# Attention scores and the folded projection as 64x32 TensorE blocks in place of half-empty 128x64 blocks

## The chip, the cores and the metric

The kernel runs on one core of a Trainium2 chip. The metric is the device time of one execution in microseconds. A kernel's time is the median of its runs, given with the lowest and the highest. Line numbers such as L177 are lines of the kernel that the profile is of, so the same statement has other numbers in other kernels.

## The reference, cut to what matters

There are 8 batches of 8 heads, 512 tokens and 32 state vectors of 64 elements each. The model has 512 columns and the hidden layer 2048. The weights come as fp64 and the kernel decodes them to fp32 itself.

```python
B, H, S, Ns, D = (8, 8, 512, 32, 64)
scores = scale * np.matmul(x, state.transpose(0, 1, 3, 2))
a = softmax(scores)                      # cut: max, exp, sum + 1e-9
xread = np.matmul(a, state)
scores2 = scale * np.matmul(state, x.transpose(0, 1, 3, 2))
a2 = softmax(scores2)
sread = np.matmul(a2, x)
# ... concatenated, heads side by side: 512 columns, then
h = x @ w_in
g = np.where(h > 0.0, h, np.exp(np.minimum(h, 0.0)) - 1.0)
return g @ w_out
```

## The kernel before

The read of the tokens is never formed. Since `xread @ w_in` is `a @ (state @ w_in)`, the kernel computes for each batch M = state x w_in (256 rows of head and state, 2048 columns) and multiplies it by the transposed softmax weights. M is made in four chunks of 512 columns; TensorE does that between the matmuls of the first feed-forward layer (`h_ps`).

Scores and M use the same stationary operand. Before the change it lay zero-padded in `k_bd`: the transposed states of four heads were put on two diagonals, so that one matmul takes all 128 partitions (two heads of 64) and 64 columns, half of which are zero for each head.

```python
def scores(b, g):
    ps = bank([P, S], "s_ps")
    for i in range(2):
        nc.tensor.matmul(ps[i * D : (i + 1) * D],
            k_bd[:, b * G + g, i * D : (i + 1) * D], st[b, g, i], ...)
    # ... two softmaxes: over the states and over the tokens

def make_m(b, c):
    m_t[b, c] = mpool.tile([P, G, 512], FP32, name="m_sb")
    for g in range(G):
        ps = bank([P, 512], "m_ps")
        for i in range(2):
            nc.tensor.matmul(ps[i * D : (i + 1) * D],
                k_bd[:, b * G + g, i * D : (i + 1) * D],
                w_in[:, 2 * g + i, c * 512 : (c + 1) * 512], ...)
        (nc.scalar.copy, nc.vector.tensor_copy)[g % 2](out=m_t[b, c][:, g], in_=ps)
# ... the main loop, for each batch b:
#     16 groups of ffn1 (h_ps), with M's chunks 1 to 3 of this batch and the attention
#     of batch b + 1 put between them,
#     then 4 groups of ffn2 (o_ps), with M's chunk 0 of batch b + 1 between them
```

`bank` takes one of three PSUM banks; `h_ps` has three of its own and `o_ps` two. At the start, the state came in 4 loads on GpSimd's queue, `x` on the sync queue and GpSimd's, and the weights on the sync queue.

Of the kernel before, what the change touches and what calls it, by code (L numbers as in the profile page):

```python
# [9 lines left out]
FP32 = mybir.dt.float32  # L10
# [9 lines left out]
def kernel(  # L20
# [11 lines left out]
    nc = tc.nc  # L32

    B, H, S, D = x.shape
    NS = state.shape[2]
    DM, DF = moe_w_in.shape
    P = 128
    R = S // P
    NP = H // 2
    G = H // 4  # L40
    FO = DF // P
    FC = DF // 512
    SB = S + NS
# [14 lines left out]
    apool = ctx.enter_context(tc.tile_pool(name="attn", bufs=2))  # L58
    xtpool = ctx.enter_context(tc.tile_pool(name="xT", bufs=4))
    atpool = ctx.enter_context(tc.tile_pool(name="aT", bufs=4))  # L60
    mpool = ctx.enter_context(tc.tile_pool(name="m", bufs=2))
    rawpool = ctx.enter_context(tc.tile_pool(name="raw", bufs=3))
    wpool = ctx.enter_context(tc.tile_pool(name="pow", bufs=2))
# [8 lines left out]
    def bank(shape, name):  # L72
        return ps_a.tile(shape, FP32, tag="a", name=name)
# [5 lines left out]
    w_in = cpool.tile([P, NP, DF], FP32, name="w_in")  # L79
    w_out = cpool.tile([P, FO, DM], FP32, name="w_out")  # L80


    v_bd = cpool.tile([P, B * G, P], FP32, name="v_bd")

    k_bd = cpool.tile([P, B * G, P], FP32, name="k_bd")

    xT_state = cpool.tile([P, NP, B * NS], FP32, name="xT_state")

# [8 lines left out]
            )  # L97

    def setup():
        nc.vector.memset(v_bd, 0.0)  # L100
        make_identity(nc, ident)
        s_v = state.rearrange("b (g h) n d -> h n (b g) d", h=4)
        for h in range(4):
            c = h % 2
            nc.gpsimd.dma_start(
                out=v_bd[h * NS : (h + 1) * NS, :, c * D : (c + 1) * D], in_=s_v[h]
            )
        for b in range(2):
            load_x(b)
        for k in range(0, B * G, 4):  # L110
            ps = bank([P, 4, P], "k_ps")
            for i in range(4):
                nc.tensor.transpose(ps[:, i], v_bd[:, k + i], ident)  # L113
            nc.vector.tensor_copy(out=k_bd[:, k : k + 4], in_=ps)  # L114

    def load_weights(dst, src):

# [41 lines left out]
    def load_w_out(fo):  # L159
        load_weights(w_out[:, fo : fo + 1], w_out_v[:, fo : fo + 1])  # L160

    def turn_x(b, g, i):

        ps = bank([P, R, P], "xT_ps")
        for r in range(R):
            nc.tensor.transpose(ps[:, r], x_t[b][:, r, (2 * g + i) * P : (2 * g + i + 1) * P], ident)  # L166
        st[b, g, i] = xtpool.tile([P, R * P], FP32, name="xT")
        nc.scalar.copy(out=st[b, g, i], in_=ps.rearrange("p r q -> p (r q)"))  # L168

    def scores(b, g):  # L170


        ps = bank([P, S], "s_ps")
        for i in range(2):
            nc.tensor.matmul(  # L175
                ps[i * D : (i + 1) * D],
                k_bd[:, b * G + g, i * D : (i + 1) * D],  # L177
                st[b, g, i],
                start=True,
                stop=True,  # L180
            )
        top = small.tile([P, 1], FP32, name="top")
        total = small.tile([P, 1], FP32, name="total")
        nc.vector.reduce_max(top, ps, axis=AX_X)
# [35 lines left out]
    def turn_state(b, g):  # L220
        ps = bank([P, R, P], "sT_ps")
        a = st[b, g, "a_s"].rearrange("p (r q) -> p r q", r=R)
        for r in range(R):
            nc.tensor.transpose(ps[:, r], a[:, r], ident)  # L224
        st[b, g, "aT_s"] = apool.tile([P, R, P], FP32, name="aT_s")
        nc.scalar.copy(out=st[b, g, "aT_s"], in_=ps)  # L226

    def state_read(b, g):

        ps = bank([P, 2, 2 * NS], "sr_ps")  # L230
        for i in range(2):
            for r in range(R):
                nc.tensor.matmul(  # L233
                    ps[:, i],
                    x_t[b][:, r, (2 * g + i) * P : (2 * g + i + 1) * P],
                    st[b, g, "aT_s"][:, r, i * D : (i + 1) * D],
                    start=(r == 0),
                    stop=(r == R - 1),
                )
        for c in range(2):  # L240
            rows = slice(c * D, (c + 1) * D)
            nc.vector.tensor_copy(  # L242
                out=xT_state[rows, 2 * g : 2 * g + 2, b * NS : (b + 1) * NS],
                in_=ps[rows, :, c * NS : (c + 1) * NS],
            )

    def make_m(b, c):

        m_t[b, c] = mpool.tile([P, G, 512], FP32, name="m_sb")
        for g in range(G):  # L250
            ps = bank([P, 512], "m_ps")
            for i in range(2):
                nc.tensor.matmul(  # L253
                    ps[i * D : (i + 1) * D],
                    k_bd[:, b * G + g, i * D : (i + 1) * D],
                    w_in[:, 2 * g + i, c * 512 : (c + 1) * 512],
                    start=True,
                    stop=True,
                )
            (nc.scalar.copy, nc.vector.tensor_copy)[g % 2](out=m_t[b, c][:, g], in_=ps)  # L260

    def attention(b):
        steps = []
        for g in range(G):
            steps += [lambda g=g, i=i: turn_x(b, g, i) for i in range(2)]
            steps += [lambda g=g: scores(b, g)]
        for g in range(G):
            steps += [lambda g=g: turn_tokens(b, g)]
            steps += [lambda g=g: turn_state(b, g)]
            steps += [lambda g=g: state_read(b, g)]  # L270
        if b + 2 < B:
            steps += [lambda: load_x(b + 2)]
        return steps
# [59 lines left out]
    for b in range(B):  # L333
        todo = attention(b + 1) if b + 1 < B else []
        g = {}
# [62 lines left out]
```

## Time and profile before

| What | Before |
|---|---|
| time, median of 4 runs (lowest to highest) | 932.17 us (931.69 to 932.48) |
| span of the profiled run | 931.1 us |
| steady period, from one batch's last `o_ps` matmul to the next batch's | 99.15 us, five times |
| the first batch's last `o_ps` matmul starts | 196.8 us |
| first weight decode begins, last one ends | 15.24 us, 165.4 us |

The periods are read from the starts of the `o_ps` matmuls in the trace; below, "the first batch ends" means the start of its last one. Two stages matter: up to about 165 us VectorE decodes the weights, and from there TensorE is full. So a saving on TensorE counts in the second stage only. This is the chain of waits at the start (start, duration, engine, what; SPq is the issue queue of SyncE, L95 loads x and L121 the raw weights):

```profile
0.74 0.45 SPq L95
...
2.71 0.97 SPq L95
...
3.72 2.93 SPq L121
...
6.69 11.91 DMA raw<-in_moe_w_in_dram
...
18.63 0.43 DVE power L126
```

Only four issues of x stand ahead of the weights, so the first weights are asked for at 3.72 us. In the chain of waits (start, duration, engine, what) VectorE takes up the second of the weights at 18.63 us.

### The profile page before, as it was taken

What the parts mean: (1) busy time and instruction counts of PE and PEld (TensorE: products, weight loads), DVE (VectorE), ACT (ScalarE), POOL (GpSimd) and SP (SyncE); (2) the same over time, 40 slices, a digit from 0 to 9 for tenths busy, and PEclk for the clock granted to TensorE, in tenths of its full rate; (3) what the DMA queues carried; (4) which work ended last, traced back from release to release, by engine and by line L of the source; (5) the groups of instructions that cost most, each with busy time, mean ns of one, the idle gap of its engine ahead of it and who ended that gap; (6) DMA issues with size and microseconds to landing.
All of it is one profiled execution on the core that took longest, in us unless ns stands there. A gap on an engine that the chain in (4) does not pass through costs nothing.

```text
span 931.1 us, 6560 instructions
## 1 busy us (share of the span) xinstructions
PE 872.7 (94%) x2512; PEld 401.3 (43%) x2512; DVE 363.1 (39%) x774; ACT 156.9 (17%) x290; POOL 53.1 (6%) x58
## 2 busy tenths in 40 slices
PE   1474999999999999999999999999999999999997
PEld 1331443445444444444444444454444444444673
DVE  3989999435004610272017400660036102500220
ACT  0211211123003300141004200330023101300110
POOL 3110110001000200010001000000001000000000
PEclk9966999999999999999999999999999999999999
DMA  8354242002000110002000200000000000000000
GB/s 200 109 148 153 90 136 91 23 23 46 1 23 23 25 21 23 23 0 46 23 23 0 46 23 1 23 1 1 23 24 0 1 23 23 0 1 23 23 0 23
DMA packets 25439, 35.01 MB, mean 38 GB/s; under 512 B 17857, under 2 KB 17857, under 8 KB 25409
## 3 DMA queue, kind: packets, MB, share of 16 engines
q1 hardware_dynamic: 23936, 29.89, 10.4%
q0 software_dynamic: 1472, 4.72, 2.3%
q8 instruction: 19, 0.31, 0.1%
q14 instruction: 12, 0.09, 0.0%
HBM read 25.69 MB, written 8.91 MB: 37 GB/s over the span
## 4 chain that ended last, share of the span: by engine, by line
PE 88%; DVE 8%; DMA 3%; SPq 1%; ACT 0%; issue 0%; POOL 0%; DVEq 0%; ACTq 0%
PE o_ps L315 49%; PE h_ps L290 23%; PE m_ps L253 6%; PE h_ps L303 3%; DMA raw<-in_moe_w_in_dram 3%; PE sr_ps L233 3%; PE s_ps L175 2%; PE xT_ps L166 2%; DVE power L139 1%; DVE w_in L148 1%; DVE power L126 1%; DVE raw L144 1%; PE sT_ps L224 1%; DVE power L131 1%; DVE power L135 1%; DVE w_in L151 0%
## 5 line engine op out<-in xcount | busy, mean ns | idle before, releaser
L315 PE MATMUL o_ps<-w_out,g_sb 128*128 128x512 f32 x1088 | 473.6, 594 | 0.0
L315 PEld LDWEIGHTS o_ps<-w_out,g_sb 128*128 128x128 f32 x1088 | 205.3, 190 | 263.0 <-issue 256.3
L290 PE MATMUL h_ps<-aT,m_sb 128*128 128x512 f32 x512 | 242.1, 606 | 12.8 <-DVE m_sb L260 12.6
L290 PEld LDWEIGHTS h_ps<-aT,m_sb 128*128 128x128 f32 x512 | 92.3, 193 | 123.1 <-issue 82.7
L279 ACT ACTIVATE e_sb<-h_ps 128x512 f32<-128x512 f32 (+1 forms) x144 | 82.4, 572 | 335.4 <-PE h_ps L290 295.9
L322 DVE COPY o_sb<-o_ps 128x512 f32<-128x512 f32 x17 | 11.7, 690 | 323.6 <-PE o_ps L315 323.6
L282 DVE SCALAR_TENSOR_TENSOR g_sb<-e_sb,h_ps 128x512 f32<-128x512 f32 (+1 forms) x144 | 93.7, 651 | 11.6 <-PE o_ps L315 8.6
L280 DVE TENSOR_SCALAR e_sb<-e_sb 128x512 f32<-128x512 f32 (+1 forms) x144 | 59.0, 410 | 98.4 <-ACT e_sb L279 98.4
L253 PE MATMUL m_ps<-w_in,k_bd 128*64 128x512 f32 x256 | 68.1, 622 | 1.5 <-ACT xT L168 0.8
L322 ACT COPY o_sb<-o_ps 128x512 f32<-128x512 f32 x17 | 10.0, 586 | 304.5 <-PE o_ps L315 304.5
L260 DVE COPY m_sb<-m_ps 128x512 f32<-128x512 f32 x32 | 22.0, 688 | 91.0 <-PE m_ps L253 89.5
L199 POOL TENSOR_TENSOR t_sb<-t_sb,top_t 128x512 f32<-128x512 f32 x16 | 17.8, 1115 | 570.0 <-DVE top_t L198 445.4
L233 PEld LDWEIGHTS sr_ps<-aT_s,x_sb 128*128 128x128 f32 x256 | 33.9, 209 | 10.9 <-ACT aT_s L226 6.4
L253 PEld LDWEIGHTS m_ps<-w_in,k_bd 128*64 128x64 f32 x256 | 15.8, 138 | 46.5 <-issue 35.3
L233 PE MATMUL sr_ps<-aT_s,x_sb 128*128 128x64 f32 x256 | 34.5, 292 | 1.4 <-ACT aT_s L226 1.3
L113 PE MATMUL k_ps<-ident,v_bd 128*128 128x128 f32 x16 | 3.9, 426 | 29.8 <-DVE k_bd L114 16.6
L303 PE MATMUL h_ps<-xT_state,w_in 128*128 128x256 f32 x128 | 27.8, 379 | 0.0
L168 ACT COPY xT<-xT_ps 128x512 f32<-128x512 f32 x32 | 18.6, 584 | 52.6 <-PE xT_ps L166 52.6
L166 PEld LDWEIGHTS xT_ps<-ident,x_sb 128*128 128x128 f32 x128 | 16.6, 151 | 22.5 <-issue 12.1
L303 PEld LDWEIGHTS h_ps<-xT_state,w_in 128*128 128x128 f32 x128 | 24.3, 190 | 3.7 <-issue 0.5
L166 PE MATMUL xT_ps<-ident,x_sb 128*128 128x128 f32 x128 | 21.4, 295 | 3.1 <-DVE xT_state L242 3.0
L260 ACT COPY m_sb<-m_ps 128x512 f32<-128x512 f32 x32 | 18.8, 586 | 22.9 <-PE m_ps L253 22.9
(42 smaller groups left out, 328.7 us busy)
## 6 DMA issues: line engine op xcount, KB each, us to landing
raw<-in_moe_w_in_dram SPq DMA_DIRECT2D x16, 512.0 KB, 4.2
raw<-in_moe_w_out_dram SPq DMA_DIRECT2D x16, 512.0 KB, 3.3
out_dram<-o_sb SPq DMA_DIRECT2D x16, 512.0 KB, 2.6
x_sb<-in_x_dram SPq DMA_DIRECT2D x16, 256.0 KB, 4.8
x_sb<-in_x_dram POOLq DMA_DIRECT2D x16, 256.0 KB, 5.9
v_bd<-in_state_dram POOLq DMA_DIRECT2D x4, 128.0 KB, 7.6
out_dram<-o_sb SPq DMA_DIRECT2D x8, 64.0 KB, 1.7
```

The lines of the kernel that those rows point to most:

```text
L166: nc.tensor.transpose(ps[:, r], x_t[b][:, r, (2 * g + i) * P : (2 * g + i + 1) * P], ident)
L175: nc.tensor.matmul(ps[i * D : (i + 1) * D], k_bd[:, b * G + g, i * D : (i + 1) * D], st[b, g, i], start=True, stop=True,)
L233: nc.tensor.matmul(ps[:, i], x_t[b][:, r, (2 * g + i) * P : (2 * g + i + 1) * P], st[b, g, "aT_s"][:, r, i * D : (i + 1) * D], start=(r == 0),
L253: nc.tensor.matmul(ps[i * D : (i + 1) * D], k_bd[:, b * G + g, i * D : (i + 1) * D], w_in[:, 2 * g + i, c * 512 : (c + 1) * 512], start=Tr ...
L260: (nc.scalar.copy, nc.vector.tensor_copy)[g % 2](out=m_t[b, c][:, g], in_=ps)
L279: nc.scalar.activation(out=e, in_=ps, func=AF.Exp)
L280: nc.vector.tensor_scalar(out=e, in0=e, scalar1=1.0, scalar2=None, op0=ALU.min)
L282: nc.vector.scalar_tensor_tensor(out=g[fo], in0=e, scalar=-1.0, in1=ps, op0=ALU.add, op1=ALU.max)
L290: nc.tensor.matmul(ps, m_t[b, fo // 4][:, k, fo % 4 * P : (fo % 4 + 1) * P], st[b, k, "aT"], start=(k == 0), stop=(k == G - 1),)
L303: nc.tensor.matmul(ps, w_in[:, co, fo * P : (fo + 1) * P], xT_state[:, co], start=(co == 0), stop=(co == NP - 1),)
L315: nc.tensor.matmul(ps, g[fo][:, c * P : (c + 1) * P], w_out[:, fo], start=(fo == 0), stop=(fo == FO - 1),)
L322: (nc.scalar.copy, nc.vector.tensor_copy)[c % 2](out=o_sb[:, c % 2], in_=ps)
```

## The change

The change regroups the heads by their place in the pair. The transposed states lie densely in `kT` (two heads of 64 partitions, 32 columns per batch), and each head's product is one block of 64 rows by 32 columns of TensorE's array. Eight such blocks, one for each head, fill the array. The intent is that all eight run side by side, in half of the time that the zero-padded blocks took.

```diff
-    def scores(b, g):
-        ps = bank([P, S], "s_ps")
-        for i in range(2):
-            nc.tensor.matmul(
-                ps[i * D : (i + 1) * D],
-                k_bd[:, b * G + g, i * D : (i + 1) * D],
-                st[b, g, i],
...
+    def by_state(b, name, rhs):
+        ps = [bank([P, 512], name) for g in range(G)]
+        for m in range(NP):
+            for g in range(G):
+                d = slice(g * D, (g + 1) * D)
+                nc.tensor.matmul(
+                    ps[g][m * NS : (m + 1) * NS],
+                    kT[d, m, b * NS : (b + 1) * NS],
+                    rhs[m][d],
+                    start=True,
+                    stop=True,
+                    tile_position=(g * D, m * NS),
+                )
+        return ps
+
+    def scores(b):
+        for g, ps in enumerate(by_state(b, "s_ps", [st[b, m] for m in range(NP)])):
+            softmaxes(b, g, ps)
...
     def make_m(b, c):
-        for g in range(G):
-            ps = bank([P, 512], "m_ps")
...
+        cols = slice(c * 512, (c + 1) * 512)
+        for g, ps in enumerate(by_state(b, "m_ps", [w_in[:, m, cols] for m in range(NP)])):
```

The setup of the state changes with it, and the two state reads of a batch become one:

```diff
     def setup():
-        nc.vector.memset(v_bd, 0.0)
...
-        s_v = state.rearrange("b (g h) n d -> h n (b g) d", h=4)
-        for h in range(4):
-            c = h % 2
-            nc.gpsimd.dma_start(
-                out=v_bd[h * NS : (h + 1) * NS, :, c * D : (c + 1) * D], in_=s_v[h]
-            )
+        s_v = state.rearrange("(q b) (m c) n d -> q m b n c d", q=2, c=2)
+        raw = [rawpool.tile([P, NP, P], FP32, tag="raw", name="s_sb") for q in range(2)]
+        for q in range(2):
+            for m in range(NP):
+                for b in range(B // 2):
+                    (nc.sync, nc.gpsimd)[q].dma_start(
+                        out=raw[q][b * NS : (b + 1) * NS, m].rearrange("p (c d) -> p c d", c=2),
+                        in_=s_v[q, m, b],
+                    )
         for b in range(2):
             load_x(b)
-        for k in range(0, B * G, 4):
+        for q in range(2):
...
```

More of the change, by code (lines that the diff above doesn't have):

```diff
@@ L39 @@
     NP = H // 2
-    G = H // 4
+    G = 2
     FO = DF // P
@@ L60 @@
     atpool = ctx.enter_context(tc.tile_pool(name="aT", bufs=4))
+    atspool = ctx.enter_context(tc.tile_pool(name="aT_s", bufs=1))
     mpool = ctx.enter_context(tc.tile_pool(name="m", bufs=2))
@@ L80 @@
     w_out = cpool.tile([P, FO, DM], FP32, name="w_out")
-    v_bd = cpool.tile([P, B * G, P], FP32, name="v_bd")
-    k_bd = cpool.tile([P, B * G, P], FP32, name="k_bd")
+    kT = cpool.tile([P, NP, B * NS], FP32, name="kT")
     xT_state = cpool.tile([P, NP, B * NS], FP32, name="xT_state")
@@ L99, in setup @@
     def setup():
-        nc.vector.memset(v_bd, 0.0)
         make_identity(nc, ident)
-        s_v = state.rearrange("b (g h) n d -> h n (b g) d", h=4)
-        for h in range(4):
-            c = h % 2
-            nc.gpsimd.dma_start(
-                out=v_bd[h * NS : (h + 1) * NS, :, c * D : (c + 1) * D], in_=s_v[h]
-            )
+        s_v = state.rearrange("(q b) (m c) n d -> q m b n c d", q=2, c=2)
[7 more added lines that the diff above has]
+                    )
         for b in range(2):
             load_x(b)
-        for k in range(0, B * G, 4):
-            ps = bank([P, 4, P], "k_ps")
-            for i in range(4):
-                nc.tensor.transpose(ps[:, i], v_bd[:, k + i], ident)
-            nc.vector.tensor_copy(out=k_bd[:, k : k + 4], in_=ps)
+        for q in range(2):
+            ps = bank([P, NP, P], "k_ps")
+            for m in range(NP):
+                nc.tensor.transpose(ps[:, m], raw[q][:, m], ident)
+            nc.vector.tensor_copy(out=kT[:, :, q * P : (q + 1) * P], in_=ps)
     def load_weights(dst, src):
@@ L160, in load_w_out, with turn_x, softmaxes @@
         load_weights(w_out[:, fo : fo + 1], w_out_v[:, fo : fo + 1])
-    def turn_x(b, g, i):
+    def turn_x(b, m):
         ps = bank([P, R, P], "xT_ps")
         for r in range(R):
-            nc.tensor.transpose(ps[:, r], x_t[b][:, r, (2 * g + i) * P : (2 * g + i + 1) * P], ident)
-        st[b, g, i] = xtpool.tile([P, R * P], FP32, name="xT")
-        nc.scalar.copy(out=st[b, g, i], in_=ps.rearrange("p r q -> p (r q)"))
-    def scores(b, g):
-        ps = bank([P, S], "s_ps")
-        for i in range(2):
-            nc.tensor.matmul(
-                ps[i * D : (i + 1) * D],
-                k_bd[:, b * G + g, i * D : (i + 1) * D],
-                st[b, g, i],
-                start=True,
-                stop=True,
-            )
+            nc.tensor.transpose(ps[:, r], x_t[b][:, r, m * P : (m + 1) * P], ident)
+        st[b, m] = xtpool.tile([P, R * P], FP32, name="xT")
+        nc.scalar.copy(out=st[b, m], in_=ps.rearrange("p r q -> p (r q)"))
+    def by_state(b, name, rhs):
+        ps = [bank([P, 512], name) for g in range(G)]
+        for m in range(NP):
+            for g in range(G):
[12 more added lines that the diff above has]
+            softmaxes(b, g, ps)
+    def softmaxes(b, g, ps):
         top = small.tile([P, 1], FP32, name="top")
@@ L224, in turn_state, with state_read @@
             nc.tensor.transpose(ps[:, r], a[:, r], ident)
-        st[b, g, "aT_s"] = apool.tile([P, R, P], FP32, name="aT_s")
-        nc.scalar.copy(out=st[b, g, "aT_s"], in_=ps)
-    def state_read(b, g):
-        ps = bank([P, 2, 2 * NS], "sr_ps")
-        for i in range(2):
+        if g == 0:
+            st[b, "aT_s"] = atspool.tile([P, R, G, P], FP32, name="aT_s")
+        nc.scalar.copy(out=st[b, "aT_s"][:, :, g], in_=ps)
+    def state_read(b):
+        ps = bank([P, NP, G, NS], "sr_ps")
+        for m in range(NP):
             for r in range(R):
                 nc.tensor.matmul(
-                    ps[:, i],
-                    x_t[b][:, r, (2 * g + i) * P : (2 * g + i + 1) * P],
-                    st[b, g, "aT_s"][:, r, i * D : (i + 1) * D],
+                    ps[:, m],
+                    x_t[b][:, r, m * P : (m + 1) * P],
+                    st[b, "aT_s"][:, r, :, m * NS : (m + 1) * NS],
                     start=(r == 0),
@@ L239, in state_read @@
                 )
-        for c in range(2):
-            rows = slice(c * D, (c + 1) * D)
+        for g in range(G):
+            rows = slice(g * D, (g + 1) * D)
             nc.vector.tensor_copy(
-                out=xT_state[rows, 2 * g : 2 * g + 2, b * NS : (b + 1) * NS],
-                in_=ps[rows, :, c * NS : (c + 1) * NS],
+                out=xT_state[rows, :, b * NS : (b + 1) * NS], in_=ps[rows, :, g]
             )
@@ L249, in make_m @@
         m_t[b, c] = mpool.tile([P, G, 512], FP32, name="m_sb")
-        for g in range(G):
-            ps = bank([P, 512], "m_ps")
-            for i in range(2):
-                nc.tensor.matmul(
-                    ps[i * D : (i + 1) * D],
-                    k_bd[:, b * G + g, i * D : (i + 1) * D],
-                    w_in[:, 2 * g + i, c * 512 : (c + 1) * 512],
-                    start=True,
-                    stop=True,
-                )
+        cols = slice(c * 512, (c + 1) * 512)
+        for g, ps in enumerate(by_state(b, "m_ps", [w_in[:, m, cols] for m in range(NP)])):
             (nc.scalar.copy, nc.vector.tensor_copy)[g % 2](out=m_t[b, c][:, g], in_=ps)
@@ L263, in attention @@
         steps = []
-        for g in range(G):
-            steps += [lambda g=g, i=i: turn_x(b, g, i) for i in range(2)]
-            steps += [lambda g=g: scores(b, g)]
+        steps += [lambda m=m: turn_x(b, m) for m in range(NP)]
+        steps += [lambda: scores(b)]
         for g in range(G):
@@ L269, in attention @@
             steps += [lambda g=g: turn_state(b, g)]
-            steps += [lambda g=g: state_read(b, g)]
+        steps += [lambda: state_read(b)]
         if b + 2 < B:
```

## The prediction

Four words are used in it and below. A pass is one run of the moving columns through TensorE's array; the trace has two passes for each fp32 product. A slot is the 430 ns between the starts of two full-array passes of 512 columns. An excursion is a stretch of passes in smaller blocks between full-array ones, and its toll is what it costs beyond its slots.

> **What bounds the kernel now.** I read the page's busy times first, then the slices, then the stretches of time by engine, then the chain of waits in order of time.
>
> The page, busy times and slices:
>
> ```profile
> PE 872.7 (94%) x2512; PEld 401.3 (43%) x2512; DVE 363.1 (39%) x774; ACT 156.9 (17%) x290; POOL 53.1 (6%) x58
> PE   1474999999999999999999999999999999999997
> DVE  3989999435004610272017400660036102500220
> PEclk9966999999999999999999999999999999999999
> ```
>
> From the fifth slice (93 us) TensorE (PE) is full; before that VectorE (DVE) is. The stretches of one later batch and of the start, by engine:
>
> ```profile
> 70.00:80.00 10.00, 0.81 (x2) 0.00 (x0) 9.61 (x21) 0.00 (x0) 0.00 (x0) 0.50 0.46 145
> 130.00:140.00 10.00, 10.00 (x25) 3.23 (x24) 9.91 (x24) 1.78 (x3) 0.00 (x0) 1.00 0.45 155
> 369.00:468.00 99.00, 99.00 (x289) 44.24 (x288) 30.43 (x64) 18.43 (x34) 6.04 (x6) 1.00 0.08 22
> ```
>
> The columns after the width are PE, weight load, DVE, ScalarE (ACT), GpSimd. So there are two stages: up to about 142 us DVE decodes the fp64 weights and sets the pace; after it PE never idles, DVE has two thirds of its time free, and a nanosecond off PE's sequence is a nanosecond off the time. The chain of waits repeats every 99.15 us there (batch 3's `h_ps` starts at 287.01, batch 4's at 386.16). The chain around one tiled stretch:
>
> ```profile
> 401.44 1.87 PE m_ps L253 x8
> 403.31 0.86 PE s_ps L175 x4
> 404.17 3.63 PE h_ps L290 x8
> ```
>
> and the groups that the change touches:
>
> ```profile
> L253 PE MATMUL m_ps<-w_in,k_bd 128*64 128x512 f32 x256 | 68.1, 622 | 1.5 <-ACT xT L168 0.8
> L175 PE MATMUL s_ps<-xT,k_bd 128*64 128x512 f32 x64 | 20.1, 641 | 1.6 <-ACT xT L168 1.6
> ```
>
> 622 ns is a latency, not what one costs. I took starts of single matmuls from the trace. An fp32 matmul is two passes. Full-array passes of 512 columns start 430 ns apart. In an M stretch the passes start at 413.658 and 413.665, then 414.138 and 414.145, 414.567 and 414.574, 414.997 and 415.003: the two 64-column blocks of a pair run together, 7 ns apart. So today M (8 passes) is 4 slots of 430 ns and scores of one group (4 passes) are 2 slots.
>
> Around each such excursion there is a toll: entry takes 522 instead of 430 ns (+92), its first pass waits for its weights (643 against 592 ns, +51), the second block starts 7 later, the exit takes 523 (+93), and the next full pass waits for its weights (697 against 592, some +100). About 0.343 us per excursion.
>
> **What the Trainium skill says.** "TensorEngine Tiling (Array Packing)", section Tiling Modes: 64x32 gives 8 independent tiles, and changing the mode drains the array; the +92 and +93 ns agree. Its section Restrictions and Gotchas: two row tiles may not write one PSUM bank together; the new code gives each half of a pair its own bank. "TensorE: Matmul & The Clock Gate", section Part 3: a packed group takes one matmul plus some 4 ns per further tile, measured up to 16 tiles at 10.6 times; it also says matmuls start strictly in program order. The trace shows 7 ns per block, and disagrees on order: in the compiled program each block's two passes stand next to each other, yet the second block's first pass starts (413.665) before the first block's second (414.138). This matters: with strict order, eight blocks of two passes would take nine slots. The same page, LDWEIGHTS (loading the stationary operand): columns / 1.2 ns, so 53 for 64 and 107 for 128; the trace's +51 and +105 agree, and 27 for 32 columns is an estimate from it.
>
> **The change part by part.**
>
> (1) Slots. M becomes 8 blocks of 64x32, two passes each, all in different tiles. If all eight run together, M is 2 slots instead of 4, and the scores of a batch 2 instead of 2x2. Per batch of the steady stage: before 4 M (16) + 2 scores (4) = 20 slots = 8.60 us; after 4x2 + 2 = 10 slots, if nothing is split.
>
> (2) Excursions. The order in which the built programs' instructions stand shows five of them per steady batch before (one joins M and scores) and six after: three whole Ms, the scores by themselves, and one M split into its first block and the other seven with an `h_ps` between. A single block still needs 2 slots, so the split adds them: 12 slots = 5.16 us. The toll of one is 0.343 - 0.024 (shorter weights) + 0.042 (six more blocks at 7 ns) = 0.361.
> Before: 8.60 + 5 x 0.343 = 10.32 us. After: 5.16 + 6 x 0.361 = 7.33 us. Gain 2.99 us.
>
> (3) A new wait. The two score banks now fill at once, and the next M needs two of the three banks of that pool after one `h_ps` of 4 passes only. Its second bank is the first score bank, which is free when ACT's exponential has read it. With scores starting at 0: `h_ps` before it ends at 0.1, ACT's ELU at 0.7, DVE's minimum and g at 1.7, DVE's maximum at 2.4, transpose issued 2.3, negated maximum 3.0, exponential 3.05 to 3.74 (durations 0.60, 0.43, 0.69, 0.69, 0.71, 0.15, 0.69 from the timeline). PE arrives there at 1.03 (scores over) + 0.10 + 4 x 0.43 + 0.09 = 2.94. So M's second block waits some 0.85 us, and I find 0.15 more at the transpose of the state weights that takes the second score bank. About 1.0 us per batch is given back. The state read in one run of 32 passes instead of two of 16 saves one entry, 0.1.
> Net per steady batch 2.99 - 1.0 + 0.1 = 2.1 us, over five such batches 10.4 us.
>
> (4) The last batch's period has only four Ms: before 16 x 0.43 + 4 x 0.343 = 8.25, after 8 x 0.43 + 4 x 0.361 = 4.88: 3.4 us.
>
> (5) Batch 0. Up to about 142 us DVE paces, so PE's saving is mostly idle time there. Of the excursions behind that point I count 7 with some 20 slots (11.0 us) before, and 8 with 16 slots (9.8 us) after: 1 us.
>
> (6) Start. Removed: memset of `v_bd` (1.77 us of DVE, beside the wait for the first weights, free), two of four copies of 0.6 us (on DVE's path: 1.2 us). Added: 32 small state loads for 4. On the sync queue 16 issues at some 0.4 us (0.315 to 0.44 is what small ones take) stand ahead of x and the weights, and two of the three raw buffers are held until the state is transposed. The first decode starts at 15.24 us now and the second weights come at 18.63; I estimate the first at about 17.5, the following close behind, with both k copies already done. Two fewer state copies per batch give DVE 0.4 us each. Net about 1 us better, plus or minus 3, since the batch-2 loads of x also stand differently among the weight loads, where DVE loses some 4.5 us today (50 to 76 us).
>
> Sum: 10.4 + 3.4 + 1 + 1 = 15.8 us. 932.2 - 15.8 = 916.4; I say 916.
>
> **The rivals.**
> *Strict order or a short look-ahead.* The trace proves only that one waiting pass can be overtaken; eight blocks need up to seven. With pairs only, M takes about 8 to 9 slots, a steady batch 41 slots and more: 17.9 + 2.2 = 20 against 10.3 us, some +60 us in all, 990. For it: the skill's sentence on order. Against: the 7 ns starts, and its 16-tile measurement. 7%.
> *Only column tiles or only row tiles run together.* Four slots per M: 22 slots and six excursions, 11.6 us, +1.3 and the bank wait per batch: about 944. 6%.
> *No bank wait.* If DVE and ACT serve the scores sooner than my walk says, 5 us more come: 911. The single place where my working is finest is this 0.85 us.
> *More bank wait.* DVE now gets both softmaxes of a batch in a burst (about 8.6 us of DVE work within some 13 us, with ELU at 1.1 us per 1.72 between); a further 1 us per batch at `h_ps`, waiting for g to free its bank, would make 921.
> *The start.* The state loads could delay everything by 5 us (921), or the weight loads could fit better (912).
>
> **Range and chances.** The PE sum is arithmetic on slots that the trace repeats to the nanosecond; the uncertain terms are the bank wait (0 to 2 us, five times), the start (plus or minus 4) and whether eight run together. The 2% line is at 913.5, 2.5 us below my number. So: range 907 to 929, chance faster 0.34, same 0.59, slower 0.07.
>
> **What would show it.** In a steady batch the period should fall from 99.15 to about 97. The trace should show eight first passes within some 50 ns, the eight second passes one slot later, and an M excursion near 0.96 us from first start to exit instead of 1.87. PE should show a new idle, on ACT's `a_s` reading `s_ps` (L204), just under 1 us per batch. The first weight decode should start at 16 to 19 us. PE should still be 90% busy or more from 100 us on. I am wrong if first passes come in twos or fours with slots between them, if PE's idle per batch exceeds 2 us, or if the stage paced by DVE ends more than 4 us from where it does.

## The result, and the profile after

| What | Before | After | Predicted |
|---|---|---|---|
| time, median | 932.17 us | 921.51 us (920.38 to 922.14, 4 runs) | 916 (907 to 929) |
| ratio to before, 95% interval | | 0.9885 [0.9868, 0.9902] | |
| span of the profiled run | 931.1 us | 919.6 us | |
| steady period | 99.15 us | 97.01 us | 99.15 - 2.1 = 97.05 |
| interval of the second batch | 89.63 us | 87.40 us | |
| last interval | 88.60 us | 86.05 us | |
| the first batch's last `o_ps` matmul starts | 196.8 us | 200.7 us | about -1 |
| first weight decode | 15.24 us | 19.81 us | 17.5 (16 to 19) |
| last weight decode | 165.4 us | 168.9 us | within 4 us |

A ratio is the mean time of one kernel's runs over that of the other's of the same rounds, so it is not quite the ratio of the medians quoted beside it.

The kernel is 1.1% faster, inside the range, 5.5 us above the number. The interval of the ratio lies below 1, but the gain is under 2%; its class, and that of every experiment below, is "same", to which the prediction gave 0.59. All outputs are right. The spans add up so: +3.9 us until the first batch's end, -2.23 in the second batch's interval, five times -2.14, -2.55 in the last, nothing in the tail (60.4 us in both), in all -11.6 with rounding, against 931.1 - 919.6 = 11.5.

The page after, busy times and slices (tenths of each fortieth of the span):

```profile
PE 860.6 (94%) x2824; PEld 392.7 (43%) x2824; DVE 359.6 (39%) x755; ACT 156.5 (17%) x290; POOL 58.1 (6%) x70
PE   4185889999999999999999999999999999999997
DVE  1979999616102720183007500570027102600220
PEclk9565989999999999999999999999999999999999
```

The shape is the same, but VectorE's first slices now read 1 and 9 instead of 3 and 9: the decoding starts later. The stretch of a steady batch, and the two of the stage before it, by engine (columns as in the prediction):

```profile
70.00:80.00 10.00, 8.90 (x26) 2.65 (x24) 9.86 (x22) 2.38 (x4) 0.00 (x0) 0.52 0.48 153
130.00:140.00 10.00, 10.00 (x25) 4.07 (x24) 9.86 (x21) 1.19 (x2) 1.91 (x2) 1.00 0.79 210
369.00:466.00 97.00, 96.91 (x330) 43.08 (x329) 30.57 (x62) 18.29 (x34) 5.93 (x6) 1.00 0.08 22
```

VectorE still paces the first stage and TensorE the second, and the granted clock of the steady stretch is 1.00 as before. The groups of the changed matmuls, by form:

```profile
L177 PE MATMUL m_ps<-w_in,kT 64*32 64x512 f32 x512 | 54.4, 620 | 2.1 <-DVE w_in L151 1.0 <-ACT m_sb L264 0.7
L177 PE MATMUL s_ps<-xT,kT 64*32 64x512 f32 x128 | 12.9, 678 | 1.4 <-ACT xT L168 1.4
```

There are twice as many passes, each as long as before (620 against 622 ns for M), and yet the busy time fell from 68.1 to 54.4 us and from 20.1 to 12.9. They overlap. One M in the order of time on TensorE:

```profile
388.99 0.59 PE L293 MATMUL h_ps<-aT,m_sb 128*128 128x512 f32 x1
389.51 1.09 PE L177 MATMUL m_ps<-w_in,kT 64*32 64x512 f32 x16
390.54 0.33 PE L166 MATMUL xT_ps<-ident,x_sb 128*128 128x128 f32 x1
```

Sixteen passes take 1.02 us from the first start to the next full-array pass; eight took 1.87. Inside, the first passes of the eight blocks start at 389.515, .522, .529, .536, .542, .548, .556 and .562, and the second passes at 389.969 to 390.016 in the same steps. So all eight blocks run together.

The chain of waits around the scores, where the new wait was expected:

```profile
298.49 1.73 PE h_ps L293 x4
300.22 0.02 issue
300.25 0.60 ACT e_sb L282
...
301.34 0.69 DVE g_sb L285
302.02 0.60 DVE top L196
302.62 0.62 DVE t_sb L201
...
303.38 0.79 ACT a_s L204 x2
304.17 0.04 issue
304.21 1.09 PE m_ps L177 x14
305.30 1.91 PE h_ps L293 x4
```

The chain leaves TensorE: the score banks are read by VectorE and then by ScalarE (`a_s`), and only when that is done, at 304.17, can M use the bank. The first block of this M started at 303.07 and its second pass at 303.53. The other seven blocks started from 304.21 on; 7 ns behind the first would have been 303.08, so they are 1.13 us late. The busy column hides this (96.91 of 97.00), because the lone block's passes count as busy; it shows in the starts and in the chain alone.

The start, from the chain of waits (L104 are the small state loads):

```profile
0.74 0.37 SPq L104
...
7.74 0.43 SPq L104
...
8.22 3.39 DMA x_sb<-in_x_dram
...
12.81 10.01 DMA raw<-in_moe_w_in_dram
...
22.84 0.43 DVE power L126
```

Sixteen issues of some 0.43 us each, 7.44 us in all, stand on the sync queue before x. The first raw weights are issued at 11.33 us instead of 3.72, and VectorE takes up the second of them at 22.84 instead of 18.63. From the first decode to the end of the last, VectorE then has less to do than before (140.4 us busy against 143.8, read from the starts and ends in the traces) but stands idle for longer (8.7 us against 6.3, mostly before raw weights).

### The profile page after: what moved, and what is told of

The parts are those of the page before. It is cut to its first block, busy times and chain, and to the rows that moved or that the text cites. A ratio compares the mean times of both kernels' runs of the same rounds, so it can differ in the third digit from the quotient of the medians. Undisturbed runs are those within 1.5% of the kernel's fastest.

```text
span 919.6 us, 7252 instructions
## 1 busy us (share of the span) xinstructions
PE 860.6 (94%) x2824; PEld 392.7 (43%) x2824; DVE 359.6 (39%) x755; ACT 156.5 (17%) x290; POOL 58.1 (6%) x70
## 4 chain that ended last, share of the span: by engine, by line
PE 84%; DVE 9%; DMA 3%; ACT 1%; SPq 1%; issue 0%; POOL 0%; DVEq 0%; ACTq 0%; POOLq 0%
PE o_ps L318 50%; PE h_ps L293 22%; PE m_ps L177 4%; PE h_ps L306 3%; DMA raw<-in_moe_w_in_dram 3%; PE sr_ps L246 3%; PE xT_ps L166 1%; DVE power L139 1%; DVE w_in L148 1%; DVE power L131 1%; DVE power L126 1%; DVE g_sb L285 1%; SPq L104 1%; PE sT_ps L236 1%; DVE raw L144 1%; DVE power L135 1%
## 5 line engine op out<-in xcount | busy, mean ns | idle before, releaser
L293 PEld LDWEIGHTS h_ps<-aT,m_sb 128*128 128x128 f32 x512 | 94.3, 195 | 132.9 <-issue 89.6
L283 DVE TENSOR_SCALAR e_sb<-e_sb 128x512 f32<-128x512 f32 (+1 forms) x144 | 63.9, 444 | 92.7 <-ACT e_sb L282 92.7
L177 PE MATMUL m_ps<-w_in,kT 64*32 64x512 f32 x512 | 54.4, 620 | 2.1 <-DVE w_in L151 1.0
L236 PE MATMUL sT_ps<-ident,a_s 128*128 128x128 f32 x64 | 11.3, 306 | 20.7 <-DVE a_s L218 19.9
L166 PE MATMUL xT_ps<-ident,x_sb 128*128 128x128 f32 x128 | 23.8, 315 | 4.6 <-ACT xT L168 2.4
L166 PEld LDWEIGHTS xT_ps<-ident,x_sb 128*128 128x128 f32 x128 | 17.5, 160 | 23.2 <-issue 10.0
L177 PEld LDWEIGHTS m_ps<-w_in,kT 64*32 64x32 f32 x512 | 8.2, 107 | 37.0 <-issue 23.6
```

What stands on the lines that cost most here:

```text
L166: nc.tensor.transpose(ps[:, r], x_t[b][:, r, m * P : (m + 1) * P], ident)
L177: nc.tensor.matmul(ps[g][m * NS : (m + 1) * NS], kT[d, m, b * NS : (b + 1) * NS], rhs[m][d], start=True, stop=True, tile_position=(g * D, ...
L236: nc.tensor.transpose(ps[:, r], a[:, r], ident)
L283: nc.vector.tensor_scalar(out=e, in0=e, scalar1=1.0, scalar2=None, op0=ALU.min)
L293: nc.tensor.matmul(ps, m_t[b, fo // 4][:, k, fo % 4 * P : (fo % 4 + 1) * P], st[b, k, "aT"], start=(k == 0), stop=(k == G - 1),)
```

## The experiments

My theory after the result was that the steady stage did as I said and that the start is the term that was mis-sized, because of the small loads. The rivals were that the steady stage gave less than its sum and the start was harmless, or that the delay came from the raw buffers which the state holds. Twelve kernels ran, in four sets, each compared with runs of the kernel before (medians 932.25, 931.95, 931.91 and 931.91 us). The last three sets ran on one chip and share most of these runs; the first ran on another chip.

### 1. The setup of before with the new blocks

```diff
-                    kT[d, m, b * NS : (b + 1) * NS],
+                    k_bd[d, b * G + m // 2, (m % 2 * 2 + g) * NS : (m % 2 * 2 + g + 1) * NS],
 # setup(): v_bd, k_bd, their memset, the 4 loads and the 4 copies as in the kernel before
```

> The changed kernel with the setup of the kernel before: state loaded by four transfers into block-diagonal tiles, 16 transposes, and the 64x32 blocks cut out of those. Theory A (the 5.5 us that my prediction missed lie in the new setup: 32 small state loads ahead of x and of the weights): the last weight decode ends at 164 to 166 us as in the kernel before, not at 168.9, and the time falls by 3 to 5 us, to 917 to 918. Theory B (batch 0 is slower because both softmaxes of a batch now come together and x is released later, whatever the setup): decode still ends at 168 or later, the time stays at 921 to 922. The period of a steady batch stays 97.0 us under both.

Measured: 916.79 us (915.65 to 918.02), ratio 0.9834 [0.9818, 0.9849]. The first decode starts at 13.28 us, the last ends at 164.7, the first batch ends at 197.2, and the period is 97.01 us as in the changed kernel. From its chain of waits (L120 loads the raw weights):

```profile
3.69 2.27 SPq L120
6.01 10.80 DMA raw<-in_moe_w_in_dram
16.83 0.43 DVE power L125
```

So the new setup alone cost 4.7 us by the medians (3.5 between the two profiled runs, 919.6 and 916.1), and the steady gain does not need it.

### 2. The sync queue relieved

```diff
-                    (nc.sync, nc.gpsimd)[q].dma_start(
+                    (nc.scalar, nc.gpsimd)[q].dma_start(
```

> The 16 state loads of the sync queue moved to ScalarE's queue, which has nothing to do at the start; the other 16 stay on GpSimd's. If what delays the start is that x and the weights stand behind 16 issues on the sync queue: first weight decode at 14 to 16 us instead of 19.8, last one at 165 to 166, time down 3 to 4 us to 918. Rival (it is the two raw buffers held by the state, or GpSimd's 16 issues ahead of its half of x): decode still starts at 18 or later, time within 1 us of 921.5.

Measured: 918.95 us (917.44 to 922.02), ratio 0.9859 [0.9835, 0.9883], period 97.01 us. The first decode starts at 12.3 us, earlier than in any other kernel here, and the last ends at 166.6 instead of 168.9. The stretch from 2 to 9 us by engine (after the clock come the busy share of the 16 DMA engines and GB/s) shows why. First the kernel before, then the changed kernel, then this one:

```profile
2.00:9.00 7.00, 0.00 (x0) 0.00 (x0) 1.00 (x1) 0.02 (x1) 5.90 (x9) 1.00 1.17 222
```

```profile
2.00:9.00 7.00, 1.34 (x3) 0.54 (x3) 0.00 (x0) 0.02 (x1) 6.91 (x15) 1.00 0.27 62
```

```profile
2.00:9.00 7.00, 0.83 (x2) 0.36 (x2) 0.00 (x0) 0.00 (x0) 6.91 (x15) 1.00 1.06 204
```

While the sync queue issues its sixteen small loads, the DMA engines are 0.27 busy and move 62 GB/s. With those issues on ScalarE's queue they move 204, close to the kernel before's 222. The delay is issue time, not bytes. This brings back 2.6 of the 4.7 us by the medians; the last decode is still 1.9 us later than with the setup of before. The trace shows a candidate for the rest: the first raw weights are issued at 7.63 us but the second only at 14.63, after this wait of the sync queue:

```profile
SPq L121 <- DMA s_sb<-in_state_dram: 6.0, 1, 6.0
```

The second load needs a raw buffer that the state still holds, and its decode begins at 19.43. How much of the time this costs was not tested.

### 3. The state in buffers of its own

```diff
-        raw = [rawpool.tile([P, NP, P], FP32, tag="raw", name="s_sb") for q in range(2)]
+        raw = [cpool.tile([P, NP, P], FP32, name=f"s_sb{q}") for q in range(2)]
```

> The state in buffers of its own, so that all three raw buffers are free for weights from the start; the queue's order as in the changed kernel. If holding two raw buffers delays the start: the second and third weight loads go out right behind the first, the 1.7 us wait before the second decode goes, time down 1.5 to 3 us. Rival (the first load is issued at 11.3 us and everything follows from that): time within 1 us of 921.5.

Measured: 921.0 us (920.24 to 922.48), ratio 0.988 [0.9859, 0.9901]. First decode 19.63 us, last 168.9. Nothing moves (the wait before the second decode stays, 1.78 us), so with this order of the queue the raw buffers held by the state are not the cause. In the prediction I had named them beside the queue. With the queue relieved they may count, as the wait in experiment 2 shows; the two edits together were not run.

### 4. Column tiles alone

```diff
-                    kT[d, m, b * NS : (b + 1) * NS],
-                    rhs[m][d],
+                    kT[g][:, m, b * NS : (b + 1) * NS],
+                    rhs[m],
...
-                    tile_position=(g * D, m * NS),
+                    tile_position=(0, m * NS),
 # kT: two zeroed tiles, each filled on one half of its partitions
```

> The regrouping kept, row tiles given up: each 32-column block uses all 128 rows, the other half of its weights zero, so only four column tiles exist and eight blocks share them. Theory (the gain of the change is that eight tiles run at once, and each tile takes its passes in turn): an M stretch is 4 slots again, first passes in two groups of four one or two slots apart; steady period up by 10 slots of 0.43 = 4.3 us less what of the bank wait is hidden, to 100.5 to 101.3; time 941 to 946, above the kernel before. Rival (the regrouping or the smaller setup gives the gain, not the row tiles): 921 to 923.

Measured: 947.16 us (946.64 to 949.07), ratio 1.0161 [1.0142, 1.018]; period 100.62 us, last interval 88.62. The chain of waits of this kernel shows the two kinds of excursion:

```profile
397.88 1.88 PE m_ps L180 x16
...
406.37 1.87 PE s_ps L180 x16
```

With 128x32 blocks sixteen passes take 1.88 us, as eight of 128x64 did. The period fell within the expected 100.5 to 101.3; the time came out 1 us above the expected range. Its first batch ends 2.1 us later than in the changed kernel, which the expectation did not have in it. So four blocks side by side give what two wider ones gave, and 32 columns alone gain nothing; the gain came only where the two halves of 64 partitions ran beside each other too. Blocks of 64 partitions without the narrow columns were not run.

### 5. The two banks one after the other

```diff
-        for m in range(NP):
-            for g in range(G):
+        for g in range(G):
+            for m in range(NP):
```

> The eight blocks issued bank by bank (four blocks of the upper rows, then four of the lower) instead of alternating. Theory (each tile keeps its own turn, any issue order packs equally): M stays near 0.97 us from first start to exit, period within 0.2 of 97.0, time 920 to 923. Rival (weights of one row group can only be loaded beside the other's stream, so alternation matters): M grows by a tenth of a us or more and the time to 925 or more.

Measured: 920.52 us (920.33 to 921.15), ratio 0.9873 [0.9857, 0.9888], period 97.0. Which of these two orders the eight blocks are issued in makes no difference; the wait for the bank is as long (the M there takes 2.14 us instead of 1.02).

### 6. The scores in other banks

This takes away the 1.13 us wait: from batch 2 on, the scores use the two banks of `o_ps`, which the first feed-forward layer does not use.

```diff
-        ps = [bank([P, 512], name) for g in range(G)]
+        ps = [tile([P, 512], name) for g in range(G)]
...
+        def free(shape, name):
+            return ps_o.tile(shape, FP32, tag="o", name=name)
+        # scores: free if b >= 2 else bank
```

> The two score banks of batches 2 to 7 come from the pool of the output banks, which is idle then, so that M never waits for the exponential that reads the scores. If the 1.13 us between the first and the second block of that M (303.08 to 304.21) is this wait and nothing else ends it: the second block follows 7 ns after the first, the period falls from 97.0 to 95.8 or 95.9, the time by 5 to 6 us to 916. Rival: another wait takes its place (DVE's g that frees a bank of h_ps, or the copy of M before it is used), and less than 0.5 us per batch comes: time 919 or more.

Measured: 923.7 us (922.89 to 923.95), ratio 0.9909 [0.9893, 0.9924]. The period is 97.02 us: nothing gained. The M behind the scores now takes 1.02 us instead of 2.15, as meant, but TensorE waits elsewhere. Its waits from 230 to 640 us, four batches (us in total, times, longest):

```profile
PE h_ps L297 <- DVE g_sb L289: 2.1, 4, 0.5
PE sT_ps L240 <- DVE a_s L222: 1.7, 4, 0.4
```

The same view of the changed kernel lists no wait at all in this stretch. The rival was right: the wait for the bank had covered two others. By the starts of the passes around these two waits, 0.58 and 0.59 us per batch are lost there, which is the 1.13 again; the view counts idle time only. The second batch's interval grew by 2.4 us (89.8 against 87.4) and the median by 2.2; the intervals of the two ratios just overlap.

### 7. The split M kept whole

In TensorE's order one M of each batch is split, one block before an `h_ps` group and seven behind it, and the lone block's stretch takes 0.99 us. This pins the first block behind the `h_ps` before it:

```diff
-                nc.tensor.matmul(
+                block = nc.tensor.matmul(
...
+                if name == "m_ps" and b and not (m or g):
+                    tc.keep_in_program_order(block)
```

> The order alone: from batch 1 on, the first block of each M is held behind the h_ps that precedes it in the program, so that no M is split into one block and seven. A lone block costs two slots and a toll: 0.86 + 0.34 = 1.20 us per steady batch. Theory: period 97.0 to 95.8, time down 6 us to 915.5. Rival: the order was chosen by the scheduler to bridge a wait, and holding M back shows that wait again: half of it or less comes, 918.5 or more.

Measured: 925.34 us (924.55 to 927.5), ratio 0.9927 [0.9913, 0.9941]. The period fell to 96.17 us, by 0.84 and not by the expected 1.2. But the interval of the second batch grew from 87.4 to 96.17, since the pin also moved that batch's attention out of the stage in which TensorE has idle time (from 140 to 170 us TensorE is busy for 20.15 us here, and for 28.65 in the changed kernel). As a version it is a loss. As a measurement it is not clean, since the pin moved part of an `o_ps` group too: by the starts in one batch the passes of M take 0.98 us less (5.21 against 6.19), and 0.22 of it comes back at the `o_ps` passes. So the split is worth 0.84 us per batch in this order.

### 8. Setup of before, other banks and whole M together

```diff
+                    k_bd[d, b * G + m // 2, ...]            # as in 1
+        ps = [tile([P, 512], name) for g in range(G)]      # as in 6
+                    tc.keep_in_program_order(block)        # as in 7
```

> All three together: old setup, score banks from the output pool, M kept whole. If the three causes are independent, -4 -5.5 -6 = -15.5 us: 906, period 94.6, 2.8% below the kernel before. If the bank wait and the split overlap or a further wait appears (softmax chain on DVE, h_ps waiting for g), 909 to 912.

Measured: 920.62 us (918.93 to 922.43), ratio 0.9875 [0.9859, 0.9891]; period and second interval 96.16 us, last decode 163.6. That is a plain miss of both expected times. Setup and banks together bring 4.7 us over experiment 7 (925.34 to 920.62), which is what the setup brought in experiment 1; the banks again bring nothing per batch (96.17 to 96.16).

### 9. VectorE relieved

If the chain behind the scores is long because VectorE has much to do there, moving work to ScalarE should shorten it:

```diff
-        nc.vector.tensor_scalar(out=a, in0=a, scalar1=total, scalar2=None, op0=ALU.mult)
+        if b >= 2:
+            nc.scalar.activation(out=a, in_=a, func=AF.Copy, scale=total)
+        else:
+            nc.vector.tensor_scalar(out=a, in0=a, scalar1=total, scalar2=None, op0=ALU.mult)
...
-            (nc.scalar.copy, nc.vector.tensor_copy)[g % 2](out=m_t[b, c][:, g], in_=ps)
+            (nc.scalar.copy, nc.vector.tensor_copy)[g % 2 if b == 0 or c != 2 else 0](out=m_t[b, c][:, g], in_=ps)
```

> VectorE relieved in the burst after the scores: from batch 2 on the state weights are scaled on ScalarE, and both halves of the third M of a batch are copied by ScalarE; banks and setup as in the changed kernel. This order keeps every M whole (five excursions), without any pin. Theory (what gave the gain back is DVE's chain through the two softmaxes that come together; the bank wait is one face of it): the split's 1.2 us goes, the 1.13 us wait for the exponential stays, since maximum and g still stand ahead of it on DVE: period 95.7 to 95.9, time 915 to 916. Rival (ScalarE, now with the scaling and the copy, becomes what M and h_ps wait for): period 96.5 or more, 919 or more.

Measured: 918.29 us (917.27 to 918.71), ratio 0.9847 [0.9832, 0.9861]; period 96.52 us, where 95.7 to 95.9 was expected. No M is split any more in the trace, which should be worth the 0.84 of experiment 7; part of it comes back as a wait of the state transposition for `a_s`, now scaled on ScalarE, 1.8 us over four batches. That is the rival's kind of wait, and its mark for the period (96.5 or more) is met, though not its mark for the time. The wait for the bank is still there (that M takes 2.15 us).

### 10. VectorE relieved, and the scores in other banks

```diff
+            nc.scalar.activation(out=a, in_=a, func=AF.Copy, scale=total)   # as in 9, with its copies of M
+        ps = [tile([P, 512], name) for g in range(G)]                      # as in 6
```

> The relief together with the score banks out of the output pool. The score banks alone left the period at 97.02, because the h_ps that waits for g, and the transpose that waits for the scaled weights, took the place of the bank wait. Theory: with DVE's chain some 2 us shorter those waits go too, so both steps together give 1.2 + 1.1 us: period 94.6 to 94.9, time 909 to 911. Rival: the chain of DVE and ScalarE is still as long as PE's work beside it, period 95.5 or more.

Measured: 919.76 us (918.62 to 920.28), ratio 0.9862 [0.9842, 0.9882]; period 96.52 us again, where 94.6 to 94.9 was expected: a miss. The waits of the same stretch:

```profile
PE sT_ps L243 <- ACT a_s L223: 3.7, 4, 0.9
PE h_ps L300 <- DVE g_sb L292: 1.9, 4, 0.5
```

Against experiment 9 the bank wait of 1.13 us per batch is gone, but the wait for `a_s` has doubled (from 1.8 to 3.7 us in four batches) and one of 1.9 us for `g_sb` has come.

### 11. The same with the setup of before

```diff
+                    k_bd[d, b * G + m // 2, ...]            # as in 1, on top of 10
```

> The relief, the score banks, and the setup of the kernel before. If the setup's 4.7 us and the period's gain add up: 905 to 907, about 2.8% below the kernel before. If not: where the first kernels differ in batch 0, up to 910.

Measured: 916.58 us (915.67 to 917.09), ratio 0.9828 [0.9814, 0.9843]; period 96.53 us. The expected 905 to 907 was a plain miss, for the reason that experiment 10 shows. The setup is worth 3.2 us here.

### 12. More TensorE work between scores and state transposition

The last run tried to fill the waits with work: two empty steps after the scores put three groups of `h_ps`, instead of one, between M and the first state transposition.

```diff
         steps += [lambda: scores(b)]
+        steps += [lambda: None] * (2 if b >= 2 else 0)
 # on top of experiment 11
```

> The kernel with the setup of before, the scores of batches 2 to 7 in their own banks and the scalings and copies of the relief on ScalarE, and now also two empty steps after the scores of each batch from the third on, so that in TensorE's order the first state transposition comes three groups of h_ps (six products) after the M blocks instead of one. Theory: what is left between the steps is a chain of latency (scores, VectorE, GpSimd, ScalarE, state transposition) that finds too little TensorE work beside it; with the work placed there no wait on a_s and none of half a microsecond on g_sb stays, the period falls from 96.5 to 94.6-95.0 us (97.01 minus 1.20 for the split M pass minus 1.13 for the bank wait), and the time to 909-911. Rival: VectorE or ScalarE are themselves the bound around the scores, so another wait (h_ps on g_sb) comes at once: period 96 or more, time 915 or more.

Measured: 917.92 us (916.4 to 918.81), ratio 0.9842 [0.9826, 0.9857]; period 96.96 us. The rival was right and my theory fell: the wait for `a_s` is gone, and TensorE waits longer than before at `h_ps`. Its waits over the four batches:

```profile
PE h_ps L300 <- ACT m_sb L270: 4.6, 4, 1.1
PE h_ps L300 <- DVE g_sb L292: 2.6, 4, 0.7
```

The chain of waits tells what is in front of them:

```profile
303.33 0.60 DVE top_t L213
...
304.07 1.06 POOL t_sb L214
...
305.15 0.63 ACT t_sb L215
305.77 0.96 ACT m_sb L270 x2
306.74 0.51 ACT e_sb L289
...
309.37 1.98 PE h_ps L300 x4
```

ScalarE stands before its exponentials `t_sb` until GpSimd has subtracted the maximum (1.06 us idle before the first, 0.16 before the second, which is the one in this chain). Behind it, in ScalarE's order, come the two copies of M and the ELU's exponential, which TensorE's next groups need. So the service of the scores by the other engines, one after the other, holds up the copies and ELUs behind it. The two copies of M on ScalarE are part of my own relief (experiment 9); whether the empty steps would do better without it was not run, and stays open.

## Why the prediction was right or wrong

- **Slots and excursions (terms 1 and 2): right.** All eight blocks run together; the first passes lie within 47 ns, and the strict-order rival is out. The excursion takes 1.02 us, where I said near 0.96. A block's first pass takes 614 ns and its second 589, so 25 for the weights, where I had estimated 27. Six excursions per batch with one M split is what the trace has. Experiment 4 shows that column tiles alone do not give it: that rival had a period of 100.62 us. Row tiles alone were not run.
- **The new wait (term 3): right in kind and nearly in size.** TensorE came to the bank when I said (2.93 us after the start of the scores, I had 2.94), but the second block could start only at 4.07: the exponential ran from 3.24 to 3.93 instead of from 3.05 to 3.74, and the read of its sum ended at 4.02. The wait is 1.13 us, where I had 0.85, and the 0.15 at the second bank's transposition was not seen: 1.13 against 1.0 in all. I expected it as idle time of TensorE, which it is not in the busy column. Net per steady batch 2.14 us against 2.1; five periods give 10.7 against 10.4. Some of this closeness is luck: without the wait the gain would be 2.14 + 1.13 = 3.27 us, where I had 2.99 + 0.1 = 3.09, so both parts were too small and the errors cancel.
- **What that wait is worth: not what I would have said.** The rival "no bank wait" put it at 5 us for the kernel. Removing it (experiments 6 and 10) gave 0.0 us per batch, since other waits on the same chain took its place.
- **The last batch and batch 0 (terms 4 and 5): right in sum by luck.** I had 3.4 + 1 = 4.4 us; the second and the last interval gave 2.23 + 2.55 = 4.8. The last batch's period has three Ms in the trace and not four, since its chunk 0 is made in the period before; three quarters of my 8.25 - 4.88 are 2.53, and 2.55 came. Against that, the second batch's interval alone has three excursions with 14 slots before and four with 8 after, at my own prices 7.05 and 4.88 us, so 2.2 us where term 5 had 1 in all. What batch 0 gains before its end is not shown: with the old setup it ends 0.4 us later than before.
- **The start (term 6): the step that failed.** I took it as "Net about 1 us better, plus or minus 3". The first batch ends 3.9 us later instead, and experiment 1 puts the setup's cost at 4.7 us. So this term was off by some 5 us, which is nearly the whole miss of 5.5; without it my sum gives 917.4, and experiment 1, with the setup of before, measured 916.79. My own rival "The start" had named this outcome, 921. The rival "More bank wait" had the same number, but its wait at `h_ps` is not in the trace. I had the issues at some 0.4 us each, sixteen of them, and that was right (7.44 us). What I failed to do was carry it through: sixteen issues push the raw weights' issue from 3.72 to 11.33 us, while the DMA engines stand at 0.27, so the first decode comes at 19.81 us, not at 17.5. I also counted all the work that VectorE is spared as time won. It is spared 3.5 us (before, four state copies stood between 31.9 and 35 us, among the decodes; now the two that are left are done before the first decode), but it stands idle 2.4 us longer, 1.7 of it before raw weights, so that the decoding takes 149.1 us instead of 150.1. The end of the decoding came 3.5 us late (4.6 from the start, less 1.1), inside the 4 that I had set as a limit, which was set too wide to be a test.
- **Signs and readings that failed.** The first decode is later than 16 to 19 us, and TensorE is not 90% busy from 100 us on: its slices from 92 to 138 us read 8. Two readings of the kernel before were loose: TensorE does idle after 142 us (busy 9.16 and 9.33 us of the ten from 140 and from 150), and VectorE's loss from 50 to 76 us was 3.8 us and not 4.5. Neither changes the account above.

The version to keep is the new blocks with the setup of before (916.79 us, ratio 0.9834, interval [0.9818, 0.9849]). Its interval lies below that of the changed kernel. The one with relief and other banks too (916.58) is not told apart from it and has more in it.

## What to carry to other kernels

Blocks that use half of the array's partitions were worth pairing with blocks that use the other half here, and the steady gain could be worked out beforehand from the starts of single passes, within 0.2 us per batch. A new layout pays for its operand too: count the issues of its loads on the queue that the first critical transfer needs, and follow that transfer's start time, not only the sum of the work. When a wait is taken away, look where the engine would wait next before counting the gain; where several engines serve one result in turn, the next wait may be as long.

## What the Trainium skill lacked or had wrong

- "TensorE: Matmul & The Clock Gate", section Part 3: Packing small matmuls — row/col tiling, says that matmuls start and end in program order. In these kernels the two passes of an fp32 block stand next to each other in the program, and all eight first passes (389.515 to 389.562) start before the first of the second passes (389.969). Up to seven waiting passes are overtaken. The trace bears out that a block's passes stand together: where one block is split off, both of its passes (408.521 and 408.974) run before the `h_ps` group that separates it from the other seven.
- The same section gives about 4 ns per further tile. Here it is 7 ns (389.515 to 389.562 is 47 ns for seven steps).
- "TensorEngine Tiling (Array Packing)", section Tiling Modes, says that a change of mode drains the array but gives no figure. In the kernel before the pass before an excursion takes 522 ns instead of 430 and the one at its end 523; after the change 523 and 519. A lone block costs as long an excursion (0.99 us) as all eight (1.02 us).
- "DMA: Bandwidth & Descriptors", section Issuing engines are not separate DMA queues, calls the time to start a DMA usually small beside the DMA. For loads of 16 KB here it was 0.43 us of the queue each against 1.8 us from issue to landing, and sixteen of them on one queue left the DMA engines at 0.27 busy; on another queue than the weights' the share was 1.06.
- No page that I found says that a wait inside a packed group is invisible in TensorE's busy time: the 1.13 us at the bank stand in a stretch that reads 96.91 of 97.00 us busy.
